# Attention and a feed-forward block in nine chunks: an earlier turn of the numerators, later operand splits

## The chip, the cores and the metric

The kernel runs on one core of a Trainium2 chip. The metric is device time in microseconds, from one launch to its end; lower is better. Inputs and outputs lie in device memory, and all arithmetic is in 32-bit floating point.

## The reference

Attention with two kinds of mask, followed by a layer norm, a feed-forward block and a residual:

```python
scores = scale * np.matmul(q, k.transpose(0, 1, 3, 2))      # 8 batches, 8 heads, 576 positions, 64
mask_local = (rel >= 0) & (rel < 32)                         # heads 0 to 3
mask_strided = (rel >= 0) & (pos[None, :] % 32 == pos[:, None] % 32)   # heads 4 to 7
attn = softmax(np.where(masks, scores, -1e9))
x = matmul(attn, v)                                          # as 8 x 576 x 512
xn = (x - mu) / np.sqrt(var + 1e-06) * g_ln
out = x + np.maximum(xn @ w_ch1, 0.0) @ w_ch2                # 512 -> 2048 -> 512
```

## The kernel before

**Chunks.** The 8 x 576 positions are worked on as nine chunks of 512, numbered 0 to 8. The feed-forward block has 16 feature blocks of 128. A factor of a matmul is kept as a high and a low part, so that a product costs three matmuls (high by high, high by low, low by high). Chunk 0 is computed while the weights are still being prepared, by a list of steps (`ORDER`). Chunks 1 and 2 are `plain`: for each feature block `f`, eight plus four matmuls into the PSUM tile `ph`, then ACT's `hh` (high part of the rectified sum), DVE's `hl` (low part), and *groups*, the second product, one group of three matmuls for each 128 positions, into the output banks `po`. Groups of a block run during the next block. The four output tiles of a chunk are two PSUM tiles of two outputs each; at a chunk's end DVE's four `finish` operations (line 901) scale and add them to the residual, and the next chunk takes the same banks. Chunks 3 to 6 are computed by `pair`: two feature blocks and two halves of the positions form a 2 x 2 block product, done with seven products (`a11 b11`, `s2 t2`, `s1 t1`, `a12 b21`, `s3 t3`, `a22 t4`, `s4 b22`), each of six matmuls of 256 columns, with a group behind each. The four sums of them (`u2`, `u3`, `p1`, line 1285) are made by DVE, and `Quarter` makes their rectified high (ACT) and low parts (DVE, `hq`). Eight pairs are one chunk. Chunks 7 and 8 end the kernel.

**Attention beside it.** A `Pair` is two heads of one batch, local or strided in turn. Its steps are woven into chunks 1 to 6, one *visit* for each pair of heads. In a visit TensorE computes the scores of the next pair (`nxt`) and the products with v of the present one (`now`); both use the same two PSUM tiles, `m` and `n`. DVE adds the mask and takes the maximum, POOL subtracts it (`s_sub`), ACT takes the exponent (`s_exp`). The result, the *numerators*, must be turned before it can be a matmul's factor: `p_turned` transposes blocks of 32 x 32 on DVE and writes them to device memory (`pd`) by four DMAs from SP, and `p_load` fetches them back as `pt`, by four DMAs from SP for strided pairs and one from ACT for local ones. The next visit's products with v read `pt`. Further steps of a visit: `v_store` writes the attention output (`xdl`, `xds`), `x_raw` fetches it back in blocks (`xraw`, from ACT), `load_v` fetches v for the pair after next, `t_piece` turns raw q and k (two transposes on DVE), and `load_qk` fetches the next raw q and k (`raw`, eight DMAs from SP, into the one tile that `t_piece` reads).

**What sets the order.** Each engine, and each DMA queue (SP's above all), does its instructions strictly in the order in which the program writes them. In chunks 1 and 2 the generator `pieces` cuts a visit in steps by `yield`; `plain` asks for four steps in each feature block, between `hl` of this block and the groups. So the first four steps of a visit stand in one block, the next four in the following one, and a visit takes three blocks (the last of a chunk takes four). In chunks 3 to 6 `pair` writes the steps out by hand between its products; the names P1, P6, P5, P2, P7, P4, P3 are the places behind the seven products, in that order. `events` does there what `X_AT` lists in the last pair (`last`) of chunks 3, 4 and 5: `x_split` makes the high (ACT) and low part (engine by `LO`) of each operand of the next chunk, as soon as its tile is free. An odd pair also turns raw q and k by `t_pieces`, one half at each `next(turns, None)`.

Of the kernel before, what the change touches and what calls it, by code (L numbers as in the profile page):

```python
# [63 lines left out]
def kernel(  # L64
# [10 lines left out]
    nc = tc.nc  # L75
# [235 lines left out]
    def bank(name):  # L311
        pool, tag, n = banks[n_bank[0] % len(banks)]
        n_bank[0] += 1
        return pool.tile([P, n], F32, tag=tag, name=name)
# [381 lines left out]
    def m_piece(p, nxt):  # L696

        name = (p or nxt).id
        ps = bank(f"m{name}"), third[0].tile([P, CH], F32, tag="h", name=f"n{name}")
        visits[0] += 1  # L700
        parts = nxt.s_blocks(ps) if nxt else None
        av = p.v_blocks(ps) if p else None
        if nxt:
            nxt.s_mask(parts)
        if p:
            p.v_divide(av[0:2])
        if nxt:
            nxt.s_max()
            nxt.s_sub()
            nxt.s_exp()  # L710
        if p:
            p.v_divide(av[2:])
            p.v_store()
# [16 lines left out]
    pairs = [Pair(b, hp) for b in range(B) for hp in order]  # L730
# [46 lines left out]
    def stage_x(name):  # L777
        if name not in staged_x:
            staged_x[name] = tkp.tile([P, 2, HC], F32, tag="tk", name=f"staged_{name}")
        return staged_x[name]  # L780

    def stage_sums(j):

        for out, x, y in (("t3", "b22", "t1"), ("t1", "t1", "b11"), ("t2", "b22", "t1"), ("t4", "b21", "t2")):
# [2 lines left out]

    OPERANDS = ("b11", "t2", "t1", "b21", "t3", "t4", "b22")
    LO = dict(b11=nc.vector, t2=nc.gpsimd, t1=nc.vector, b21=nc.gpsimd, t3=nc.gpsimd, t4=nc.gpsimd,
              b22=nc.vector)  # L790
    xs = {}

    def x_hi(name):
# [2 lines left out]
    def x_lo(name, eng=None):  # L796
        hi, lo = xs[name]
        (eng or LO[name]).tensor_tensor(out=lo, in0=stage_x(name), in1=hi.bitcast(F32), op=ALU.subtract)
        if name == "t4":
            del staged_x[name]  # L800

    def x_split(name):
        x_hi(name)
        x_lo(name)
# [292 lines left out]
    def pieces(i0, i1):  # L1097
        for i in range(i0, i1):
            now = pairs[i] if i >= 2 * NHP else None
            nxt = pairs[i + 1]  # L1100
            short = i not in (3 * NHP - 1, i1 - 1)
            soon = not nxt.local
            m_piece(now, nxt)
            yield
            yield
            yield
            yield
            if now and i < 4 * NHP:
                now.x_raw(nc.scalar)
            nxt.p_turned()  # L1110
            yield
            nxt.v_sums()
            if soon:
                nxt.p_load((nc.sync,))
            pairs[i + 2].load_v()
            yield
            pairs[i + 2].t_piece()
            yield
            pairs[i + 3].load_qk()
            yield  # L1120
            if not soon:
                nxt.p_load((nc.scalar,))
            yield
            if now and (now.b == 2 or i in (3 * NHP + 2, 3 * NHP + 3)):
                now.x_blocks()
            yield
            yield
            yield
            if not short:
                for _ in range(4):  # L1130
                    yield
# [139 lines left out]
    def product2(p, name, x, ps, start=True):  # L1271
        if name in slots:
            w = slots[name]
        else:
            w = high1[p] if name == "a22" else w1s[2 * p][:, :, HC * (int(name[2]) - 1):HC * int(name[2])]
        xh, xl = xs[x]
        for j in range(2):
            wh, wl = (w[:, i, P * j:P * (j + 1)] for i in range(2))
            for i, (wx, xx) in enumerate(((wh, xh), (wh, xl), (wl, xh))):
                nc.tensor.matmul(  # L1280
                    ps, wx, xx[:, j], start=(start and j == 0 and i == 0), stop=(j == 1 and i == 2),
                    skip_group_check=not start)
# [20 lines left out]
    def late_low():  # L1303
        if late:
            late.pop().low()
# [50 lines left out]
        (7, "P5"): [lambda: half_x(0, "b210", G, in_a(2))],  # L1356
        (7, "P7"): [lambda: half_x(0, "b211", V, (xb_t[1][:, 0], xb_t[1][:, 1]))],
    }
    X_AT = dict(P1=("b11",), P6=("t2",), P2=("b21",), P7=("t3",), P4=("t1", "t4"), P3=("b22",))

    def pair(c, p):
        even, last = p % 2 == 0, p == NFC // 2 - 1
        fin, entry = c == wide - 1, (c, p) == (FIRST, 0)
        n = NFC * (c - FIRST) + 2 * p
        i = NHP * (c + 1) + 1 + p // 2
        now, nxt, soon, far = (pairs[k] if k < NP else None for k in range(i, i + 4))
        off = 3

        def events(slot):
            if fin:  # L1370
                for do in final.get((p, slot), ()):
                    do()
            elif last:
                for name in X_AT.get(slot, ()):
                    x_split(name)

        if even and now:
            ps = bank(f"m{i}"), ps_b.tile([P, CH], F32, tag="h", name=f"n{i}")
            parts = nxt.s_blocks(ps) if nxt else None
            av = now.v_blocks(ps)  # L1380
            now.v_divide(av[0:2])
            if nxt:
                if not nxt.local:
                    parts[0:2] = parts[1], parts[0]
                nxt.s_mask(parts)
            now.v_divide(av[2:])
            now.v_store()
            if nxt:
                nxt.s_max()
        late_low()  # L1390
        if entry:
            x_lo("b22")
        x1 = ps_h.tile([P, CH], F32, tag="h", name=f"x1_{c}_{p}")[:, 0:HC]
        product2(p, "a11", "b11", x1)
        nc.scalar.copy(out=p1_t, in_=x1)
        events("P1")
        split_w(n + 1)
        if even and nxt:
            nxt.s_sub()
            if not entry:  # L1400
                nxt.s_exp()
        elif nxt:
            nxt.v_sums()
            nxt.p_load((nc.scalar, nc.sync))
        stage_w(n + 3)
        run_groups(1)
        x2 = ps_b.tile([P, CH], F32, tag="h", name=f"x2_{c}_{p}")[:, 0:HC]
        product2(p, "s2", "t2", x2)
        add2(u2_t, x2, p1_t)
        if entry:  # L1410
            x_lo("t4", nc.vector)
        turns = soon.t_pieces() if soon and not even else iter(())
        next(turns, None)
        if p == 1:
            pairs[NHP * (c + 1)].x_raw(nc.sync)
        events("P6")
        run_groups(1)
        x3 = bank(f"x3_{c}_{p}")[:, 0:HC]
        product2(p, "s1", "t1", x3)
        next(turns, None)  # L1420
        events("P5")
        run_groups(1)
        product2(p, "a12", "b21", x1, False)
        q = Quarter(c, 2 * p, 0, x1)
        q.low()
        split_w(n + 2)
        w_whole(NFC // 2 * (c - FIRST) + p)
        if entry:
            nxt.s_exp()
        elif even and nxt:  # L1430
            nxt.p_turned()
        stage_w(n + 4)
        events("P2")
        run_groups(1)
        product2(p, "s3", "t3", x2, False)
        add2(u3_t, x2, p1_t)
        add2(p1_t, x3, u3_t)
        q22 = Quarter(c, 2 * p + 1, 2, p1_t)
        if entry:
            nxt.p_turned()  # L1440
        if even and soon:
            soon.load_v()
        if even and now and p < NFC // 2 - 2:
            now.x_raw(nc.scalar, range(2))
        if far and not even:
            far.load_qk()
        events("P7")
        run_groups(1)
        x4 = (ps_h if even else ps_b).tile([P, CH], F32, tag="h", name=f"x4_{c}_{p}")[:, 0:HC]
        product2(p, "a22", "t4", x4)  # L1450
        add2(u3_t, x4, u3_t)
        q21 = Quarter(c, 2 * p + 1, 0, u3_t)
        q22.low()
        if 0 <= p - off < NT:
            res[c].append([x_load(c, p - off)])
        if even and now and p < NFC // 2 - 2:
            now.x_raw(nc.scalar, range(2, 4))
        if now and not even and not last:
            now.x_blocks()
            if p == 5 and not fin:  # L1460
                stage_sums(1)
        events("P4")
        run_groups(1)
        product2(p, "s4", "b22", x3, False)
        add2(u2_t, x3, u2_t)
        late.append(Quarter(c, 2 * p, 2, u2_t))
        q21.low()
        if 0 <= p - off - 1 < NT:
            k = p - off - 1
            res[c][k].append(x_scale(res[c][k][0], f"{c}_{k}"))  # L1470
        if p == 3:
            pairs[NHP * (c + 1)].x_blocks()
            if not fin:
                stage_sums(0)
        events("P3")
        run_groups(2)
# [99 lines left out]
    for f in range(NFC):  # L1576
# [4 lines left out]
        if f in (5, 6, 8, 9):  # L1581
            i = (5, 6, 8, 9).index(f)
# [5 lines left out]
    last = {}  # L1588
# [39 lines left out]
```

## Time and profile before

| | before |
|---|---|
| median of 3 runs | 884.07 us (881.9 to 884.26) |
| the profiled execution's own time | 882.23 us |
| its span | 880.4 us |
| TensorE busy | 860.8 us, 98% of the span |
| VectorE (DVE) busy | 555.0 us, 63% |
| ScalarE (ACT) busy | 282.8 us, 32% |
| GpSimd (POOL) busy | 369.9 us, 42% |

The span goes from the first to the last instruction. Busy time is not the same as useful time: matmuls overlap, so that a matmul that starts a little late may leave no gap in the busy time. Rows of a timeline give start and duration in us, the engine, the line of the kernel, the operation, the tile written and the tiles read, and, in brackets, how long the engine stood idle before and what ended that. Rows of waits give the total in us, the count, and the longest.

### The profile page before, as it was taken

How to read it: one execution, taken by the hardware profiler on the slowest of the kernel's cores; microseconds unless marked ns; L12 is line 12 of the kernel's file. 1: busy time of each engine (PE TensorE's matmuls, PEld its weight loads, DVE VectorE, ACT ScalarE, POOL GpSimd, SP SyncE). 2: the span in 40 equal slices, each digit the busy share in tenths (PEclk: the TensorE clock that was granted, in tenths of full speed). 3: DMA queues.
4: the chain of work that ended last, by engine and by line, in shares of the span. 5: the costliest groups of instructions: out<-in, count | busy, mean ns of one | idle time of the engine just before them, and what ended most of it. 6: DMA issues, size and time to landing. Idle time of an engine off the chain costs nothing.

```text
span 880.4 us, 20783 instructions
## 1 busy us (share of the span) xinstructions
PE 860.8 (98%) x7981; PEld 729.7 (83%) x7981; DVE 555.0 (63%) x1161; ACT 282.8 (32%) x588; POOL 369.9 (42%) x444
## 2 busy tenths in 40 slices
PE   6799999999999999999999999999999999999997
PEld 6678888888788888888888888888888888888886
DVE  6799994555555568676766776677866852434442
ACT  3686741111111114233432342334334421212121
POOL 4777852433333335245624452456437711212000
PEclk9799999999999999999999999999999999999999
DMA  9999853768868777979698978886774124321111
GB/s 189 189 293 273 249 110 88 154 161 168 169 169 158 181 167 177 215 183 190 164 207 196 194 175 209 182 172 157 174 176 118 49 96 137 102 85 48 55 41 48
DMA packets 374746, 137.99 MB, mean 157 GB/s; under 512 B 297204, under 2 KB 353144, under 8 KB 374648
## 3 DMA queue, kind: packets, MB, share of 16 engines
q1 hardware_dynamic: 317016, 125.00, 58.6%
q10 hardware_dynamic: 57632, 11.67, 7.2%
q8 instruction: 63, 1.03, 0.5%
q14 instruction: 35, 0.29, 0.1%
HBM read 99.58 MB, written 37.03 MB: 155 GB/s over the span
## 4 chain that ended last, share of the span: by engine, by line
PE 79%; DMA 7%; DVE 5%; SPq 4%; issue 2%; ACT 1%; POOL 1%; ACTq 1%; DVEq 0%; POOLq 0%
PE po L927 37%; PE x L1280 15%; PE x L1507 9%; PE ph L878 8%; PE ph L885 4%; PE m L454 2%; DMA pt<-pd 1%; SPq L362 1%; PE n L523 1%; DMA v_s<-in_v_dram 1%; SPq L651 1%; DMA xraw<-xds 1%; PE m L523 1%; DVE u L1285 1%; PE t L379 1%
## 5 line engine op out<-in xcount | busy, mean ns | idle before, releaser
L927 PE MATMUL po<-w,hq 128*128 128x512 f32 x768 | 213.7, 394 | 0.0
L927 PE MATMUL po<-w,hh 128*128 128x512 f32 x640 | 199.5, 393 | 0.0
L927 PEld LDWEIGHTS po<-w,hq 128*128 128x128 f32 x768 | 129.8, 189 | 14.3 <-issue 0.3
L927 PEld LDWEIGHTS po<-w,hh 128*128 128x128 f32 x640 | 118.1, 188 | 24.4 <-issue 0.2
L927 PE MATMUL po<-w,hl 128*128 128x512 f32 x320 | 124.8, 390 | 0.0
L1280 PE MATMUL x<-xh_b,w 128*128 128x256 f32 x512 | 113.1, 284 | 0.9 <-DVE u L1285 0.8
L1280 PEld LDWEIGHTS x<-xh_b,w 128*128 128x128 f32 x512 | 87.3, 188 | 10.9 <-DVE u L1285 5.7
L1222 POOL TENSOR_TENSOR w<-sw,w 128x256 fp32r<-128x256 f32 x64 | 52.1, 835 | 77.4 <-ACT w L1221 58.6
L895 DVE SCALAR_TENSOR_TENSOR hl<-ph,hh 128x512 fp32r<-128x512 f32 x48 | 33.0, 687 | 77.8 <-ACT hh L890 77.6
L500 POOL TENSOR_TENSOR sm<-sm,mx 128x640 f32<-128x640 f32 (+1 forms) x31 | 40.6, 1309 | 93.4 <-DVE mx L495 57.7
L878 PE MATMUL ph<-xh,w 128*128 128x512 f32 x188 | 74.6, 397 | 0.0
L753 POOL TENSOR_TENSOR rs<-rs,mhalf 128x1 f32<-128x1 f32 x36 | 22.3, 619 | 122.9 <-DVE rs L752 116.7
L878 PE MATMUL ph<-xl,w 128*128 128x512 f32 x188 | 73.4, 390 | 0.0
L1280 PE MATMUL x<-xl_b,w 128*128 128x256 f32 x256 | 71.8, 281 | 0.0
L927 PEld LDWEIGHTS po<-w,hl 128*128 128x128 f32 x320 | 60.1, 188 | 12.7
L890 ACT ACTIVATE hh<-ph 128x512 fp32r<-128x512 f32 x48 | 28.6, 597 | 115.1 <-PE ph L885 86.1
L1280 PEld LDWEIGHTS x<-xl_b,w 128*128 128x128 f32 x256 | 48.2, 188 | 4.7
L506 ACT ACTIVATE sm<-sm 128x648 f32<-128x648 f32 (+1 forms) x32 | 23.8, 744 | 84.5 <-POOL sm L500 70.3
L885 PE MATMUL ph<-xh,w 128*128 128x512 f32 x188 | 50.5, 391 | 0.0
L1172 POOL TENSOR_TENSOR rings<-stage,rings 128x512 fp32r<-128x512 f32 x14 | 18.1, 1292 | 74.5 <-ACT rings L1171 74.5
L1293 ACT ACTIVATE hq<-u 128x256 fp32r<-128x256 f32 x64 | 26.7, 417 | 60.1 <-DVE u L1285 22.0
L1222 POOL TENSOR_TENSOR xh_a<-sw,xh_a 128x256 fp32r<-128x256 f32 x32 | 24.3, 758 | 48.9 <-ACT xh_a L1221 48.9
(224 smaller groups left out, 1748.8 us busy)
## 6 DMA issues: line engine op xcount, KB each, us to landing
s<-in_moe_w_ch_dram SPq DMA_DIRECT2D x32, 512.0 KB
sw<-sd SPq DMA_DIRECT2D x64, 256.0 KB
out_dram<-x SPq DMA_DIRECT2D x32, 256.0 KB
raw<-in_q_dram SPq DMA_DIRECT2D x108, 72.0 KB
raw<-in_k_dram SPq DMA_DIRECT2D x108, 72.0 KB
xds<-xo SPq DMA_DIRECT2D x32, 162.0 KB
v_l<-in_v_dram SPq DMA_DIRECT2D x32, 144.0 KB
pd<-sm SPq DMA_DIRECT2D x48, 96.0 KB
```

The lines of the kernel that those rows point to most:

```text
L500: eng.tensor_tensor(out=sm, in0=sm, in1=mx[:, :, 0:nt].unsqueeze(3).broadcast_to([P, 2, nt, sm.shape[3]]), op=ALU.subtract)
L506: nc.scalar.activation(out=self.smv, in_=self.smv, func=AF.Exp, scale=SCALE)
L753: nc.gpsimd.tensor_tensor(out=rs, in0=rs, in1=mhalf, op=ALU.pow)
L878: nc.tensor.matmul(ph, w1h[:, cc], x[:, cc, :], start=(new and n == 0 and i == 0), stop=False)
L885: nc.tensor.matmul(ph, w1l[:, cc], xt[c][0][:, cc, :], start=False, stop=(cc == NCC - 1))
L890: nc.scalar.activation(out=hh, in_=ph, func=AF.Relu)
L895: nc.vector.scalar_tensor_tensor(out=hl, in0=ph, scalar=0.0, in1=hh.bitcast(F32), op0=ALU.max, op1=ALU.subtract)
L927: nc.tensor.matmul(po[c, i], hx, w, start=(n_po[c, i] == 0 and n == 0), stop=(n_po[c, i] == NFC - 1 and n == 2))
L1222: nc.gpsimd.tensor_tensor(out=w[:, 1], in0=t[:, k], in1=w[:, 0].bitcast(F32), op=ALU.subtract)
L1280: nc.tensor.matmul(ps, wx, xx[:, j], start=(start and j == 0 and i == 0), stop=(j == 1 and i == 2), skip_group_check=not start)
L1293: nc.scalar.activation(out=self.h[0], in_=src, func=AF.Relu)
L1507: nc.tensor.matmul(ps, wx, xx, start=(start and j == 0 and i == 0), stop=(j == 1 and i == 2), skip_group_check=not start)
```

## The change

In chunks 1 and 2 the numerators' turn and its four writes go from the visit's fifth step to its fourth, and so from the second feature block of the visit to its first. The fetch of strided numerators goes behind the v loads and one step later. In the last pair of chunks 3, 4 and 5 the second transposition of raw q and k goes from behind `s1 t1` to behind the sums that follow `s3 t3`; `t1` is split at P3 in place of P4, behind the last product; and the low part of `b22` is made by POOL in place of DVE there (at the entry to chunk 3 it stays on DVE).

```diff
     LO = dict(b11=nc.vector, t2=nc.gpsimd, t1=nc.vector, b21=nc.gpsimd, t3=nc.gpsimd, t4=nc.gpsimd,
-              b22=nc.vector)
+              b22=nc.gpsimd)
...
             yield
             yield
             yield
+            nxt.p_turned()
             yield
             if now and i < 4 * NHP:
                 now.x_raw(nc.scalar)
-            nxt.p_turned()
             yield
             nxt.v_sums()
+            pairs[i + 2].load_v()
+            yield
             if soon:
                 nxt.p_load((nc.sync,))
-            pairs[i + 2].load_v()
-            yield
             pairs[i + 2].t_piece()
...
-    X_AT = dict(P1=("b11",), P6=("t2",), P2=("b21",), P7=("t3",), P4=("t1", "t4"), P3=("b22",))
+    X_AT = dict(P1=("b11",), P6=("t2",), P2=("b21",), P7=("t3",), P4=("t4",), P3=("t1", "b22"))
...
         if entry:
-            x_lo("b22")
+            x_lo("b22", nc.vector)
...
         product2(p, "s1", "t1", x3)
-        next(turns, None)
+        if not last:
+            next(turns, None)
         events("P5")
...
         q22 = Quarter(c, 2 * p + 1, 2, p1_t)
+        next(turns, None)
```

The order of DVE in the first visit of chunk 1, one piece of the difference: L482 and L495 are mask and maximum, L633 the turn of the numerators `sm`, L901 the four `finish` of chunk 0, L895 `hl` of feature block 1.

```order
 L482 TENSOR_TENSOR sm_191<-m_2_2161,mask_s 64x54
 L495 TENSOR_REDUCE mx_2_2188<-sm_191 128x12
+L633 STREAM_TRANSPOSE sm_192<-sm_191 128x6x4x32
 L901 SCALAR_TENSOR_TENSOR x_0_1845<-po_0_992,rs_0_1888,x_0_1845 128x512
 L901 SCALAR_TENSOR_TENSOR x_1_1824<-po_0_992,rs_1_1877,x_1_1824 128x512
 L901 SCALAR_TENSOR_TENSOR x_2_1792<-po_2_999,rs_2_1818,x_2_1792 128x512
 L901 SCALAR_TENSOR_TENSOR x_3_1945<-po_2_999,rs_3_2092,x_3_1945 128x512
-L895 SCALAR_TENSOR_TENSOR hl_1_2227<-ph_1_2212,hh_1_2225 128x512
-L633 STREAM_TRANSPOSE sm_192<-sm_191 128x6x4x32
+L895 SCALAR_TENSOR_TENSOR hl_1_2232<-ph_1_2217,hh_1_2230 128x512
```

The turn has moved from behind `hl` to ahead of the four `finish`; chunk 2 begins in the same way.

The order of SP in a later visit of chunk 1 with strided scores to come, before: `xdl` is the attention output, `sd` the weight sums, `pd` the numerators' writes, `x` the residual, `pt` their fetch.

```order
L586 DMA xdl<-xo 128x4x128
L587 DMA xdl<-xo 64x128
L836 DMA sd<-f_1_2465 128x2x256
L837 DMA sd<-f_1_2468 128x512
L637 DMA pd_205<-sm_192 32x4x192 x4
L741 DMA x_1_2655<-xdl 128x256
L743 DMA x_1_2655<-xds 128x1x256
L651 DMA pt_3_2661<-pd_205 128x6x32 x4
L400 DMA v_l<-in_v_dram 32x17x64
L401 DMA v_l<-in_v_dram 32x18x64
```

The same place of SP now:

```order
L586 DMA xdl<-xo 128x4x128
L587 DMA xdl<-xo 64x128
L637 DMA pd_205<-sm_192 32x4x192 x4
L836 DMA sd<-f_1_2465 128x2x256
L837 DMA sd<-f_1_2468 128x512
L741 DMA x_1_2655<-xdl 128x256
L743 DMA x_1_2655<-xds 128x1x256
L400 DMA v_l<-in_v_dram 32x17x64
L401 DMA v_l<-in_v_dram 32x18x64
L400 DMA v_l<-in_v_dram 32x17x64
L401 DMA v_l<-in_v_dram 32x18x64
L651 DMA pt_3_2665<-pd_205 128x6x32 x4
```

The writes `pd` have passed the two `sd`, and the fetch `pt` stands behind the four v loads.

The order of DVE in the last pair of chunk 3, before: `qt_s` and `kt_s` are the two turns, `u`, `p` the sums, `hq` low parts, `xl_a` the low part of `t1`.

```order
L428 STREAM_TRANSPOSE qt_s<-raw_3_5255 128x18x32
L428 STREAM_TRANSPOSE kt_s<-raw_3_5255 128x18x32
L1296 SCALAR_TENSOR_TENSOR hq_14_0_5565<-x_3_7_5510,hq_14_0_5565 128x256
L1285 TENSOR_TENSOR u_2143<-x_3_7_5534,p_2141 128x256
L1285 TENSOR_TENSOR p_2141<-x_3_7_5548,u_2143 128x256
L1285 TENSOR_TENSOR u_2143<-x_3_7_5604,u_2143 128x256
L1296 SCALAR_TENSOR_TENSOR hq_15_2_5588<-p_2141,hq_15_2_5588 128x256
L798 TENSOR_TENSOR xl_a<-staged_3768,xh_a 128x512
L1285 TENSOR_TENSOR u_2142<-x_3_7_5548,u_2142 128x256
```

The same place of DVE now:

```order
L428 STREAM_TRANSPOSE qt_s<-raw_3_5255 128x18x32
L1296 SCALAR_TENSOR_TENSOR hq_14_0_5564<-x_3_7_5510,hq_14_0_5564 128x256
L1285 TENSOR_TENSOR u_2143<-x_3_7_5534,p_2141 128x256
L1285 TENSOR_TENSOR p_2141<-x_3_7_5548,u_2143 128x256
L428 STREAM_TRANSPOSE kt_s<-raw_3_5255 128x18x32
L1285 TENSOR_TENSOR u_2143<-x_3_7_5604,u_2143 128x256
L1296 SCALAR_TENSOR_TENSOR hq_15_2_5587<-p_2141,hq_15_2_5587 128x256
L1285 TENSOR_TENSOR u_2142<-x_3_7_5548,u_2142 128x256
L1296 SCALAR_TENSOR_TENSOR hq_15_0_5612<-u_2143,hq_15_0_5612 128x256
```

The second turn stands behind two sums, and the low part of `t1` has left the place ahead of the last sum.

## Rows read from the trace of the kernel before

**Rows 1.** Waits of PE, 140 to 345 us and 415 to 626 us.

```profile
PE n L523 <- DMA pt<-pd: 1.4, 2, 1.0
...
PE x L1280 <- DVE u L1285: 0.8, 3, 0.4
```

**Rows 2.** Timeline of PE in chunk 1: scores and first groups of two visits.

```profile
182.66 0.80 PE L454 MATMUL m<-kt_s,qt_s 64*64 64x54 f32 x40
...
184.40 0.74 PE L927 MATMUL po<-w,hh 128*128 128x512 f32 x2
...
219.24 0.80 PE L454 MATMUL m<-kt_s,qt_s 64*64 64x54 f32 x40
...
222.01 0.73 PE L927 MATMUL po<-w,hh 128*128 128x512 f32 x2
```

**Rows 3.** Chain of waits, followed back from 221 us: start, duration, what.

```profile
213.73 2.94 DMA xraw<-xds
...
216.69 4.38 DMA pt<-pd
```

**Rows 4.** Timeline of SP's DMA issues in chunk 1.

```profile
195.48 3.90 SPq L651 DMA_DIRECT2D pt<-pd  x4
199.42 0.54 SPq L400 DMA_DIRECT2D v_l<-in_v_dram  x1
...
205.21 3.03 SPq L362 DMA_DIRECT2D raw<-in_k_dram  x4
...
211.18 2.70 SPq L637 DMA_DIRECT2D pd<-sm  x4
```

**Rows 5.** Timelines of ACT and DVE in the same visit: exponent and turn.

```profile
206.42 0.74 ACT L506 ACTIVATE sm<-sm 128x640 f32<-128x640 f32 x1 [4.71 <-DMA raw<-in_q_dram]
...
209.77 0.83 DVE L633 STREAM_TRANSPOSE sm<-sm 128x640 f32<-128x640 f32 x1
```

**Rows 6.** Timelines of DVE, ACT and PE in the first visit of chunk 1.

```profile
150.04 2.72 DVE L901 SCALAR_TENSOR_TENSOR x<-po,rs,x 128x512 f32<-128x512 f32 x4
...
154.88 0.97 DVE L633 STREAM_TRANSPOSE sm<-sm 128x768 f32<-128x768 f32 x1
...
151.51 0.75 ACT L506 ACTIVATE sm<-sm 128x648 f32<-128x648 f32 x1 [3.83 <-POOL sm L500]
...
153.38 0.61 PE L927 MATMUL po<-w,hh 128*128 128x512 f32 x2
```

**Rows 7.** Timeline of PE at the end of chunk 3: groups, product, scores.

```profile
423.77 0.86 PE L927 MATMUL po<-w,hq 128*128 128x512 f32 x3
...
425.18 0.86 PE L927 MATMUL po<-w,hq 128*128 128x512 f32 x3
...
426.47 0.39 PE L1280 MATMUL x<-xh_b,w 128*128 128x256 f32 x1 [0.44 <-DVE u L1285]
...
427.29 0.86 PE L927 MATMUL po<-w,hq 128*128 128x512 f32 x3
...
428.69 1.55 PE L927 MATMUL po<-w,hq 128*128 128x512 f32 x6
...
430.35 0.80 PE L454 MATMUL m<-kt_s,qt_s 64*64 64x54 f32 x40
...
432.90 0.86 PE L927 MATMUL po<-w,hq 128*128 128x512 f32 x3
...
434.50 0.86 PE L927 MATMUL po<-w,hq 128*128 128x512 f32 x3
```

**Rows 8.** Timelines of DVE and POOL in the same place.

```profile
424.58 1.25 DVE L428 STREAM_TRANSPOSE kt_s<-raw 128x576 f32<-128x576 f32 x1
...
430.21 1.17 DVE L1296 SCALAR_TENSOR_TENSOR hq<-u,hq 128x256 fp32r<-128x256 f32 x1
...
432.31 0.68 DVE L798 TENSOR_TENSOR xl_b<-staged,xh_b 128x512 fp32r<-128x512 f32 x1
...
429.55 1.55 POOL L798 TENSOR_TENSOR xl_b<-staged_t,xh_b 128x512 fp32r<-128x512 f32 x1
```

## The prediction

> **What bounds the kernel now.** I read the page's busy shares first, then TensorE's waits, then single instructions around each wait. TensorE is busy for 98% of the span and the other engines for 63% or less, so an edit pays only where a matmul starts later than its predecessor allows. Behind the first chunk there are few such places: the waits show two for `pt<-pd` in chunks 1 and 2 (1.4 us together), and three for `u` in chunks 3 to 5 (0.8 us together) [rows 1]. Recorded waits understate the loss, since matmuls overlap, so below I compare starts: from one fixed matmul to the next, against the same distance where nothing is late.
>
> **Chunks 1 and 2: what the earlier turn saves.** In an undisturbed visit the strided scores start at 182.66 and the groups behind the visit at 184.40: 1.74 us. In the visit of the long wait it is 219.24 to 222.01, 2.77 us, so 1.03 are lost [rows 2]. The visit at 299.00 has the same pattern with 2.25 us and loses 0.51. Together 1.54 us.
>
> The chain back from that wait is `xds` store, `xraw` (ends at 216.67), local numerators `pt` from 216.69 to 221.07 [rows 3]. Its start is SP: it was still issuing `raw` loads up to 208.24 and came to the four `pd` writes only at 211.18 [rows 4]. They had been ready earlier: the exponent ended at 207.16, the turn started at 209.77, behind the next feature block's `hl` [rows 5]. Now the turn follows the exponent at once, 2.6 us earlier, and the writes stand ahead of `sd` and `xraw`. In strided visits SP no longer sits in the numerators' fetch (3.9 us for four issues, [rows 4]) while the v loads queue behind it, so the `raw` loads end earlier too and the next `xds` store and `xraw` follow. The fetch of `pt` takes 4.4 us and is late by 1.0; the turn alone gives its writes 2.6. I take the whole 1.54 us, with 0 as the other end.
>
> What is moved past: four `pd` writes go ahead of two `sd` writes, so these leave some 2 us later. They free POOL's weight-sum tiles; POOL stands idle for much of these chunks (42% busy over the span), so I cost that at nothing. It would cost something if POOL came late to a visit's subtraction, since the turn now keeps DVE waiting for it. In ordinary visits `hl` is not delayed: the turn now runs from 207.2 to 208.0, and `hl`, some 0.7 us long, ended only as the old turn began at 209.77 [rows 5]. In the visit of chunk 2 with operand transposes behind the turn the same check leaves `hl` some 0.4 us late, which the twelve matmuls of groups before its PSUM bank is written again cover.
>
> **Chunks 1 and 2: what it costs.** A chunk's first visit differs. There DVE has also the four `finish` operations, which empty the output banks of the chunk before, and they stood ahead of the turn; the order shows them behind it now. In front they ran at 150.04, four in 2.72 us, in the very time in which POOL and ACT made the exponent. Now DVE waits for the exponent (ends at 152.26), turns (0.97), and only then finishes at 0.68 each. The first group of the new chunk writes the bank of the first two: 152.26 + 0.97 + 2 x 0.68 = 154.59, where TensorE wanted it at 153.38 [rows 6]. That is 1.2 us of new wait. The next two finishes end at 155.95, and TensorE asks at 154.59 + 1.36 = 155.95: no second wait. `hl` is done some 0.7 later, before its bank is wanted. The same sum at the next chunk's first visit (a local one, turn 0.84, exponent to 250.25, groups at 251.40) gives 1.05. Together **+2.3 us**. Bounds: 0 if the groups don't wait for both finishes, 2.7 if latencies of 0.2 are added at each.
>
> **The last pair of chunks 3, 4, 5.** Both turns of the next raw tile (the second at 424.58, 1.25 us) stand ahead of DVE's `u` sums [rows 8]. The product a22·t4 writes the PSUM tile that the sum reads, and waits. From group to group with one product between it is 1.41 us undisturbed (423.77 to 425.18) and 2.11 here (425.18 to 427.29): 0.70 lost [rows 7]. Chunks 4 and 5 show the same pair of rows with 1.83 and 1.81: 0.42 and 0.40. Together 1.52. With the second turn behind both sums this goes: they are free about 1.1 us earlier, and the largest loss is 0.7. What is late next is a22's own sum, behind the turn; only the next visit's tile needs it, over 1 us later. The eight `raw` loads wait for the turn also, some 0.7 us later on SP; no one needs them for a pair.
>
> At the chunk's end, t1's low part (a wait for ACT, then 0.9) stood ahead of the sum that frees the bank for the visit's scores. They start 1.66 us after the last two groups (428.69 to 430.35), where other visits show 1.48: 0.18 lost, in each of three chunks, 0.54 together [rows 7]. b22's low part at 432.31 then delays the visit's reading, and the group-to-group distance is 1.60 (432.90 to 434.50) for 1.41: 0.19, three times, 0.57 [rows 7, 8]. With t1 behind the sum and b22 on POOL, DVE has one subtraction fewer there. Together 1.52 + 0.54 + 0.57 = **2.6 us** saved; bounds 0.5 (only part of the first) and 2.6. A gain above it is excluded, since nothing more is lost in these places. Operands are wanted later than they come: t1 in the third product of the next pair, b22 in its last.
>
> On POOL against DVE the rows speak against the move: `hq` took 1.17 us at 430.21, while the same instruction takes 0.41 to 0.42 elsewhere, and POOL was in t4's subtraction (429.55, 1.55 us) [rows 8]. The Trainium skill (SBUF — State Buffer, section "SBUF: two separate sides") says that a DVE instruction with two SBUF inputs and a GpSimd instruction that reads SBUF take a port as an exclusive lock, one blocking for all of the other's time. The trace agrees in direction (0.75 us added). By that rule t1's subtraction may now wait out one of POOL's.
>
> **The sum.** 2.3 - 1.5 - 2.6 = -1.9 us. The profiled execution's own time is 882.23 (span 880.4), so 880.3 for a like one. It lies 1.8 below the median of 884.07, within its runs (881.9 to 884.26); on the median the forecast is **882.2**. That is 0.2%. About 0.3% (2.7 us) is what a measurement of this kernel can tell from no change.
>
> **The rivals.**
> - *The chunk starts cost nothing* (the finishes stay in time, because the exponent comes sooner or one finish is enough): -4.2 us, 879.9. For it: DVE idles before `hl` there. Against it: the exponent's end is in the rows, and the bank holds two outputs. Chance 0.15.
> - *The `pt` waits stay*, because the local fetch follows `xraw` and not the writes: in the chain it starts 0.02 us after `xraw` ends [rows 3]. Then 2.3 - 2.6 = -0.3, 883.8. Chance 0.14.
> - *The last pairs gain nothing*: another reader of the same bank is late in place of the sum, as happens at 0.15 us in an odd pair that is not changed. 2.3 - 1.5 = +0.8, 884.9. The edit would not do what it says. Chance 0.10.
> - *DVE is blocked by POOL at the chunk's end*: t1's subtraction, due at about 429.9, waits out 1.5 us of POOL and ends as the visit starts; the third loss of 0.57 stays. -1.3, 882.7. Chance 0.08. This is what the SBUF page's rule would do here.
> - *Slower: strided numerators come too late.* Their fetch stands behind four v loads, each about 0.55 us of issue [rows 4], and stood ahead of them. If the writes' lead does not bring SP to it earlier, it ends 2.2 us later, and four of the five strided visits (the fifth has a feature block to spare) stall TensorE for up to that: +8.8 - 1.9, 891.0. It decides once the fetch's last issue ends later than 2 us before the products that read it; in rows 4 it ended at 199.38, and no wait of that visit is among rows 1. Against it: the turn is 2 to 3 us earlier, which pays for the v loads. Chance 0.08.
>
> **How the numbers follow.** The forecast has 0.45, the rivals 0.55 as above. The range for 8 in 10: down to the first rival and 0.6 for the spread of the runs (879.3), up to the third with a little spread (885.2); what lies outside is the slower case and the tails. Faster by over 0.3% (below 881.4): most of the first rival (0.13) and a quarter of the forecast (0.11), 0.24. Slower: the last rival and a tail, 0.09. Within: 0.67.
>
> **What would show it.** Right: no wait for `pt<-pd` in chunks 1 and 2, distances of 1.74 in all strided visits; two new waits of the first groups of chunks 1 and 2 for DVE's `finish` (line 901), 1.2 and 1.05 us; group distances near 1.41 in the last pairs, and only the unchanged pair's small wait for `u` left. Wrong: new waits for `pt` behind strided visits, `hl` late in ordinary visits, waits of DVE for POOL at chunk ends, or two starts of chunks without a gap.

## The result, and the profile after

The changed kernel takes 895.03 us, median of 6 runs (893.57 to 897.32); the kernel before took 883.42 beside it (6 runs, 880.96 to 884.26). The ratio is 1.0138, 95% interval 1.0117 to 1.0159: 12 us slower, where I forecast 2 us faster. The profiled execution took 893.57 us, 11.3 more than that of before (882.23), and its span is 891.8.

The head of the page (busy time per engine; then TensorE's busy tenths in 40 slices of the span):

```profile
PE 863.0 (97%) x7981; PEld 730.5 (82%) x7981; DVE 556.1 (62%) x1158; ACT 283.0 (32%) x588; POOL 373.0 (42%) x447
...
PE   7799999998998989999999999999999999999997
```

Apart from the first two slices and the last, TensorE's row has three below 9, all between 200 and 340 us (before it had none), so the loss lies in chunks 1 and 2 and in three places. Waits of PE from 140 to 350 us (compare the first of [rows 1]; each line gives what was waited for, us in total, times, longest):

```profile
PE n L523 <- DMA pt<-pd: 8.3, 6, 2.5
PE po L927 <- DVE x L901: 2.2, 2, 1.2
```

The second line was forecast. The first should have been empty; it has grown from 1.4 to 8.3 us, and the visits have changed: the two late ones of before had local numerators, and these go with `v_s`, so they are strided. Timeline of PE at the first two of them and at the third (start, duration, instruction, the wait ahead of it):

```profile
204.72 0.30 PE L523 MATMUL n<-v_s,pt 54*64 54x64 f32 x2 [2.17 <-DMA pt<-pd]
205.72 0.24 PE L523 MATMUL n<-v_s,pt 54*64 54x64 f32 x1 [0.58 <-DMA pt<-pd]
206.46 0.79 PE L927 MATMUL po<-w,hh 128*128 128x512 f32 x2
...
289.65 0.30 PE L523 MATMUL n<-v_s,pt 54*64 54x64 f32 x2 [2.46 <-DMA pt<-pd]
290.61 0.24 PE L523 MATMUL n<-v_s,pt 54*64 54x64 f32 x1 [0.54 <-DMA pt<-pd]
...
329.00 0.29 PE L523 MATMUL n<-v_s,pt 54*64 54x64 f32 x2 [1.84 <-DMA pt<-pd]
330.09 0.33 PE L523 MATMUL n<-v_s,pt 54*64 54x64 f32 x1 [0.67 <-DMA pt<-pd]
```

By the yardstick of the prediction (from the start of the scores to the first group, 1.74 to 1.76 in an undisturbed visit) the three take 4.88, 5.13 and 5.18 us: 3.1 + 3.4 + 3.4 = 9.9 us lost. From these scores to the next ones the three are longer than before by 4.73, 3.34 and 4.30 us, 12.4 together: another 2.4 us are lost behind two of the stalls. The granted clock shows where. Behind the first and the third, but not the second (290 to 295 us), TensorE ran part of the time at 1.2 instead of 2.4 GHz (stretches of 5 us: length, busy us of PE, PEld, DVE, ACT, POOL, then PEclk, DMA share, GB/s):

```profile
200.00:205.00 5.00, 2.83 (x84) 2.15 (x82) 0.69 (x1) 0.60 (x1) 0.00 (x0) 1.00 0.80 117
205.00:210.00 5.00, 4.42 (x52) 3.51 (x51) 2.74 (x9) 0.00 (x0) 1.10 (x1) 0.70 0.75 121
210.00:215.00 5.00, 5.00 (x22) 4.09 (x21) 1.31 (x2) 1.34 (x2) 1.56 (x3) 0.96 0.59 156
290.00:295.00 5.00, 4.46 (x58) 3.72 (x57) 2.74 (x9) 0.00 (x0) 1.21 (x1) 1.00 0.70 113
325.00:330.00 5.00, 2.58 (x82) 1.84 (x80) 0.69 (x1) 0.60 (x1) 0.31 (x1) 0.99 0.86 132
330.00:335.00 5.00, 4.91 (x52) 4.13 (x53) 2.74 (x9) 0.00 (x0) 1.25 (x2) 0.67 0.62 102
```

Why the fetch is late is in the chain of waits behind the first stall (start, duration, what; SPq is SP issuing a DMA):

```profile
190.95 2.42 DMA xraw<-xdl
...
193.44 0.38 SPq L836
...
195.51 0.53 SPq L400
...
197.16 1.93 SPq L401
...
199.13 1.13 SPq L651
...
202.44 3.15 DMA pt<-pd
```

SP had issued the `pd` writes early. Then it stood 0.8 us, until an `xraw` transfer had landed, before it issued `sd` (L836); it passed `x` and the four v loads, the last of which took 1.93 us, and began the fetch (L651) at 199.13. Before, it began at 195.48 [rows 4]. The writes and the fetch in SP's timeline, here and (last line) the writes of the kernel before:

```profile
190.56 2.04 SPq L637 DMA_DIRECT2D pd<-sm  x4
...
199.13 4.59 SPq L651 DMA_DIRECT2D pt<-pd  x4
```

```profile
192.50 1.79 SPq L637 DMA_DIRECT2D pd<-sm  x4
```

The writes left 1.9 us earlier than before, and the fetch started 3.65 us later and its four issues took 0.69 longer. (The scores of this visit start 0.64 us later than before, 201.58 against 200.94, so against them the lead is 2.6 and the delay 3.0 us.) The lead went nowhere.

At the other edits: the first groups of chunks 1 and 2 wait for `finish` (L901), as forecast (PE):

```profile
153.91 0.70 PE L927 MATMUL po<-w,hh 128*128 128x512 f32 x2 [1.17 <-DVE x L901]
...
256.87 0.70 PE L927 MATMUL po<-w,hh 128*128 128x512 f32 x2 [1.05 <-DVE x L901]
```

From the scores across a last pair to the next scores it took 24.03, 23.75 and 23.79 us before, and 23.27, 23.24 and 23.26 now: 1.80 us gained in chunks 3 to 5. The stretch behind each, with the first pairs of the next chunk, took 23.30, 23.28 and 23.31, and takes 23.42, 23.42 and 23.44 now: 0.39 lost.

### The profile page after: what moved, and what is told of

It reads as the page before. It is cut to its first block, busy times and chain, and to the rows that moved or that the text cites. A ratio compares the mean times of both kernels' runs of the same rounds, so it can differ in the third digit from the quotient of the medians.

```text
span 891.8 us, 20777 instructions
## 1 busy us (share of the span) xinstructions
PE 863.0 (97%) x7981; PEld 730.5 (82%) x7981; DVE 556.1 (62%) x1158; ACT 283.0 (32%) x588; POOL 373.0 (42%) x447
## 4 chain that ended last, share of the span: by engine, by line
PE 86%; DMA 4%; SPq 3%; DVE 2%; issue 2%; POOL 1%; ACT 1%; ACTq 0%; POOLq 0%; DVEq 0%
PE po L927 41%; PE x L1280 18%; PE x L1509 9%; PE ph L878 7%; PE ph L885 4%; PE m L454 2%; PE n L523 1%; SPq L651 1%; DMA pt<-pd 1%; PE m L523 1%; SPq L401 1%; DMA v_l<-in_v_dram 1%; POOL sm L500 1%; DMA s<-in_moe_w_ch_dram 1%; DMA pd<-sm 1%
## 5 line engine op out<-in xcount | busy, mean ns | idle before, releaser
L927 PE MATMUL po<-w,hh 128*128 128x512 f32 x640 | 201.6, 397 | 2.2 <-DVE x L901 2.2
L895 DVE SCALAR_TENSOR_TENSOR hl<-ph,hh 128x512 fp32r<-128x512 f32 x48 | 32.9, 686 | 64.1 <-ACT hh L890 64.1
```

Source lines behind the costliest of these rows:

```text
L895: nc.vector.scalar_tensor_tensor(out=hl, in0=ph, scalar=0.0, in1=hh.bitcast(F32), op0=ALU.max, op1=ALU.subtract)
L927: nc.tensor.matmul(po[c, i], hx, w, start=(n_po[c, i] == 0 and n == 0), stop=(n_po[c, i] == NFC - 1 and n == 2))
```

## The experiments

The theory after the result: the fetch's place behind the v loads alone makes the three stalls. Rivals: the early `pd` writes crowd SP and the DMA queues, whatever stands where; or `sd`, now between writes and fetch (where only `x` stood before), does it.

### The fetch put back ahead of v

```
             nxt.v_sums()
+            if soon:
+                nxt.p_load((nc.sync,))
             pairs[i + 2].load_v()
             yield
-            if soon:
-                nxt.p_load((nc.sync,))
```

> The changed kernel with one thing undone: SP again issues the strided numerators' fetch ahead of the four v loads. The early turn and the edits of the last pairs stay. Theory (the fetch stands behind v on SP and so ends late): the three waits for the numerators of 1.8 to 2.5 us go, with them about 9.9 us of late groups and about 2.5 us of lower clock behind them; what is left of the change is +2.7 (two chunk starts), -1.6 (old waits for the numerators gone), -1.3 (last pairs), so about 883 us, within 1 us of the kernel before. Rival (the early writes, ahead of the sd and x transfers, crowd the queues and make the fetch late): the stalls stay, 892 us or more.

Measured: 881.84 us (12 runs), ratio to before 0.9971, interval 0.9954 to 0.9988. Waits of PE from 140 to 350 us, and SP in chunk 1:

```profile
PE po L927 <- DVE x L901: 2.2, 2, 1.2
PE n L523 <- DMA pt<-pd: 1.0, 2, 0.6
```

```profile
194.84 3.78 SPq L651 DMA_DIRECT2D pt<-pd  x4
198.66 0.54 SPq L400 DMA_DIRECT2D v_l<-in_v_dram  x1
```

The stalls are gone and the early writes acquitted. But the fetch starts at 194.84, only 0.64 us earlier than before, though its writes left 2.7 us earlier (189.83). With `sd` in between (0.8 us of waiting for `xraw` and 0.9 us of issues), most of the turn's lead doesn't reach the fetch. That lead could not have paid for the v loads. Against the kernel before the ratio is 2.6 us of gain, where I had expected next to none; this is taken up below.

### The kernel before with the fetch alone moved

The reverse: only the fetch moves behind v, the turn stays late.

> The kernel before with one thing done: the strided fetch stands behind the four v loads; the turn stays in its late place. Theory (the place behind v makes it late): the fetch ends at least as late as in the changed kernel, since its writes leave 2 us later; three to four visits stall by 3 to 6 us each, and the time is 893 to 905 us. Rival (only early writes crowd the queues): no new wait, 883 to 885 us.

Measured: 895.13 us (4 runs), ratio 1.0127, interval 1.0101 to 1.0153. As slow as the whole change, by this one move. Waits of PE from 140 to 350 us, and SP's fetch in chunk 1:

```profile
PE n L523 <- DMA pt<-pd: 8.7, 7, 2.7
```

```profile
198.25 4.12 SPq L651 DMA_DIRECT2D pt<-pd  x4
```

The early turn bought these three visits little: scores to groups take 5.06, 4.66 and 5.83 us, much as in the changed kernel. Only the first strided visit of chunk 1 stalls here and not there (2.54 us, 0.8 lost).

### Without the v loads ahead of the fetch

In the changed kernel, `if not soon:` ahead of `pairs[i + 2].load_v()`. This kernel leaves the four v loads out, so its local pairs use old values of v and its result is not the attention; it serves for the time alone.

> The changed kernel without the four v loads that stand ahead of the strided fetch: in chunks 1 and 2, the v tiles of the local pairs keep the values of the batch before (that part of the computation is changed). Theory (the v loads' issues on SP make the fetch late): its last issue comes 3 to 4 us earlier, the three waits of 1.8 to 2.5 us go, 882 to 884 us. Rival (the sd and x transfers between the writes and the fetch, and the wait of sd for an earlier transfer, make it late): most of the stalls stay, 890 us or more.

Measured: 881.04 us (10 runs), ratio 0.9957, interval 0.9941 to 0.9974, and no wait for `pt` from 140 to 350 us. The fetch begins at 194.63 and ends its issues at 198.58:

```profile
194.63 3.95 SPq L651 DMA_DIRECT2D pt<-pd  x4
```

`sd` still stands in front of it, and the fetch still stands one step later than before. So the second rival falls too, and so does the later step: the four v loads make the stalls.

### The fetch issued by ACT

`p_load((nc.scalar,))` in place of `p_load((nc.sync,))`, at the place of the changed kernel.

> The changed kernel with the strided fetch issued by ACT instead of SP, at the same place of the program; the v loads stay on SP. Theory (only SP's order of issue makes the fetch late): it no longer queues behind v, the waits for the numerators fall to under 1 us, and ACT pays with four issues of some 0.5 us in each of five visits beside its own work, which has 283 us in 892: 881 to 884 us. Rival (v loads and fetch share the DMA engines and their transfers collide): the fetch starts earlier but takes longer, waits of 1 to 2 us stay, 886 to 892 us.

Measured: 884.88 us (10 runs), ratio 1.0005, interval 0.9986 to 1.0024. The stalls are gone here as well (0.4 us for `pt`), which confirms SP's order as the cause. The price is on ACT (its timeline) and, behind it, PE:

```profile
309.87 4.70 ACTq L651 DMA_DIRECT2D pt<-pd  x4
314.67 0.60 ACT L890 ACTIVATE hh<-ph 128x512 fp32r<-128x512 f32 x1 [7.62 <-DMA pt<-pd]
```

```profile
316.04 0.50 PE L878 MATMUL ph<-xh,w 128*128 128x512 f32 x1 [1.53 <-DVE hl L895]
```

Four issues hold ACT for 4.7 us here, so `hh` starts late, `hl` with it, and the next feature block waits. I had taken an issue at 0.5 us; in this visit it is 1.2, and over the five visits the four take 3.03 to 4.70 us. By the ratios this costs about 3 us against the fetch put back ahead of v, and the time lies just above the range of my theory.

### The turn late again at the chunk starts

The changed kernel, with `p_turned` behind the finishes for `i in (7, 12)` only.

> The changed kernel with the turn in its old place in the first visits of chunks 1 and 2 alone, behind the four finish operations. Theory (the turn ahead of the finishes costs 1.5 and 1.2 us at the chunk starts): the two waits for the finishes of 1.17 and 1.05 us go, -2.7 us against the changed kernel, 892.3 us, since the first strided visit has time to spare. Rival (the first strided visit then stalls on its fetch as the three others do, +3.3): 895.5 us.

Measured: 894.95 us (4 runs), ratio 1.0119, interval 1.0094 to 1.0145; against the changed kernel's 1.0138 no clear gain, so my theory missed. The waits for `finish` are gone, and the two stretches behind them are shorter (18.84 to 17.38 us, 19.62 to 18.31: 2.8 us). In the profiled executions more than that, 4.9 us, is given back in the other stretches of the two chunks, nearly all in the visits that read strided numerators:

```profile
PE n L523 <- DMA pt<-pd: 9.8, 7, 2.6
...
163.83 0.24 PE L523 MATMUL n<-v_s,pt 54*64 54x64 f32 x1 [0.84 <-DMA pt<-pd]
```

The first strided visit now stalls too (2.81 us from scores to groups, 1.06 lost), and the others take 5.21, 5.57 and 5.75 instead of 4.88, 5.13 and 5.18: 2.4 us more of stalls, and the other 2.5 lie behind them. My reading, which no run separates: while the transfer is the last to arrive, an earlier start of TensorE only makes it wait longer. My rival had the place right and the price too high: 1.1 us there, the rest in the other visits.

### The last pairs alone

The kernel before with the second turn behind two sums, `t1` and `b22` split later, and `b22` on POOL; and the same with `b22` on DVE.

> The kernel before with the edits of the last pairs alone (second turn behind two sums, t1 and b22 split later, b22 on POOL). Read from the two traces: -2.3 us in the last pairs, +0.9 in the first pair of the chunks behind them, so -1.3 to -1.4 us, about 882 us. Rival (the loss in the first pairs comes from somewhere else in the change, such as the shifted phase of the weights' loads): -2.3 us and no loss there, 881.2 us.

> As the edits of the last pairs alone, but b22's low part stays on DVE. Theory (b22 on POOL pushes POOL's weight split and the visit's subtraction back, and so the product s4*b22 of the next pair by 0.3 us each): that loss goes, 0.9 us; in exchange DVE has b22 there again, which in the kernel before cost 0.19 us three times (0.57). So -2.3 + 0.6 = -1.7 us against before, 0.3 us faster than with b22 on POOL. Rival (POOL has no part in it): the loss of 0.9 stays and the 0.57 comes back, -0.8 us.

Measured: 883.35 us, ratio 0.9987 (0.9964 to 1.0010), and 883.88, ratio 0.9994 (0.9975 to 1.0013), 12 runs each. The times don't separate the two from each other or from the kernel before; the stretches do:

| from scores to scores, us | across the last pairs | behind them |
|---|---|---|
| before | 24.03, 23.75, 23.79 | 23.30, 23.28, 23.31 |
| changed kernel | 23.27, 23.24, 23.26 | 23.42, 23.42, 23.44 |
| last pairs alone, b22 on POOL | 23.25, 23.24, 23.27 | 23.43, 23.44, 23.60 |
| last pairs alone, b22 on DVE | 23.27, 23.24, 23.31 | 23.72, 23.71, 23.72 |

The first column repeats: about 1.8 us, whatever else is in the kernel. In the second, both versions lose, in different places. With `b22` on POOL (changed kernel, chunk 4; POOL, ACT and PE in turn):

```profile
445.07 1.28 POOL L798 TENSOR_TENSOR xl_b<-staged,xh_b 128x512 fp32r<-128x512 f32 x1
...
448.17 1.27 POOL L500 TENSOR_TENSOR sm<-sm,mx 128x648 f32<-128x648 f32 x1
```

```profile
449.47 0.75 ACT L506 ACTIVATE sm<-sm 128x648 f32<-128x648 f32 x1 [3.44 <-POOL sm L500]
450.13 0.36 ACT L1293 ACTIVATE hq<-x 128x256 fp32r<-128x256 f32 x1
```

```profile
451.85 0.85 PE L927 MATMUL po<-w,hq 128*128 128x512 f32 x3
453.53 1.55 PE L927 MATMUL po<-w,hq 128*128 128x512 f32 x6
```

POOL does `b22` first, then the weight split, then the visit's subtraction; the exponent and `hq` follow late, and the product s4·b22 waits: 1.68 us between the groups at 451.85 and 453.53 instead of 1.41. Three chunks lose 0.27, 0.32 and 0.31 there. With `b22` on DVE (the same places of PE):

```profile
437.23 0.86 PE L927 MATMUL po<-w,hq 128*128 128x512 f32 x3
439.26 0.86 PE L927 MATMUL po<-w,hq 128*128 128x512 f32 x3
...
444.89 0.86 PE L927 MATMUL po<-w,hq 128*128 128x512 f32 x3
446.30 1.55 PE L927 MATMUL po<-w,hq 128*128 128x512 f32 x6
```

The late product is back at 1.41 (444.89 to 446.30), so POOL was its cause. But the first distance is 2.03 where it was 1.60 before [rows 7]: DVE now does `t1` and `b22` one after the other ahead of the visit's reading. I had priced that at the old 0.19; moving `t1` there made it 0.62. In both kernels the product behind that distance starts 0.14 us after DVE has read the visit's tile `n` (433.57 and 438.33), so DVE's queue ahead of the reading is the cause. Part of that queue is an `hq` that takes 1.18 us beside a subtraction of POOL, where 0.42 is usual (in the kernel before one takes 1.17 there); those 0.76 us are more than the 0.62 lost, so by this estimate POOL has a share here too, which no run separates. By the stretches, `b22` is better off on POOL, the reverse of what I expected.

### The parts that pay, together

The early turn except for `i in (7, 12)`, the fetch ahead of v, the last pairs with `b22` on POOL.

> The parts that pay, together: the turn early except in the first visits of chunks 1 and 2, the strided fetch ahead of v as before, the edits of the last pairs with b22 on POOL. Theory: the changed kernel with the fetch put back (881.8 in its run, 0.9971 of before) less 2.7 us of chunk starts: about 5 us under the kernel before, 0.994 of it, near 879.5 us, with no wait of TensorE for a finish. Rival (the early turns themselves gain nothing and the earlier run only lay well): 0.998 of before, as the edits of the last pairs alone.

Measured: 880.00 us (6 runs, 878.43 to 880.87) against 884.39 of before beside it; ratio 0.9948, interval 0.9927 to 0.9968. Faster than both kernels, and near the 0.994 that I expected. Waits of PE from 140 to 350 us:

```profile
PE n L523 <- DMA pt<-pd: 1.4, 2, 0.9
```

Two small waits for `pt` remain and none for `finish`.

### Why the early turn may be worth more than it seemed

The last pairs alone give 1.1 us by their ratio (0.9987) and all paying parts 4.6 (0.9948): so the early turn would give about 3.5 us, or 2.5 by the medians (the ratios on record are not quite the quotients of the medians), where the trace of before showed 1.5. The two ratios' intervals leave this open from about 1 to 6 us. The trace of before was a good execution (882.23 us; the medians of before in the two later series are 885.22 and 884.39). The two kernels with the last pairs alone have the program of before in chunks 1 and 2. From the first scores of chunk 1 to the first product of chunk 3 the profiled executions took:

| kernel | us |
|---|---|
| before | 191.58 |
| last pairs alone, b22 on POOL | 193.86 |
| last pairs alone, b22 on DVE | 198.70 |
| changed kernel | 205.07 |
| fetch put back (with 2.7 us of chunk starts) | 194.10 |
| the parts that pay | 191.65 |

Up to 7 us lie between executions of the same code. The slowest waits for the same local numerators as [rows 2], only for longer (PE, `b22` on DVE):

```profile
221.26 0.24 PE L523 MATMUL n<-v_l,pt 64*32 64x64 f32 x1 [2.29 <-DMA pt<-pd]
222.16 1.20 PE L927 MATMUL po<-w,hh 128*128 128x512 f32 x2
```

Its first groups behind the stall take 1.20 us, where [rows 2] has 0.73 and 0.74: the lower clock again (granted 0.72 from 220 to 225 us). In the six profiled executions with the early turn no wait at a local visit of chunks 1 and 2 is over 0.5 us; but the kernel with the fetch alone moved, whose turn is late, has none either, so the turn is not the only thing that removes them. The six runs of the last kernel lie within 2.4 us, the 23 of before beside it within 7.0 (881.49 to 888.46). Why the transfers differ from run to run isn't settled.

## Why the prediction was wrong, and where it was right

| term of the sum, us | forecast | changed kernel |
|---|---|---|
| waits for local `pt` go | -1.5 | -1.56 |
| two chunk starts | +2.3 | +2.7 |
| strided fetch behind v | 0 (rival: +8.8) | +9.9, and +2.4 of clock |
| across the last pairs | -2.06 | -1.80 |
| behind the last pairs | -0.57 | +0.39 |
| ahead of chunk 1 (not changed) | 0 | -0.8 |

The measured terms sum to 11.2; the profiled executions differ by 11.3.

- **The step that failed** is the sentence "the turn is 2 to 3 us earlier, which pays for the v loads". The writes did leave 1.9 us earlier. But the same move that put them ahead of `sd` put `sd` between them and the fetch, with 0.8 us in which SP stood until an `xraw` transfer had landed. I asked what the writes' move does to `sd` and POOL, and never what `sd` does to the fetch. With the fetch put back, the lead that arrives is 0.64 us, against 3.6 us for four v loads (195.51 to 199.09 in the chain). I had taken 2.2, read where the loads stood behind the fetch; ahead of it the fourth one takes longer.
- **The slack was in my own rows.** I wrote that it decides 2 us before the products that read the fetch, and that the last issue ended at 199.38. Those products stood 0.9 us behind the scores at 200.94 (PE, kernel before):

```profile
201.84 0.27 PE L523 MATMUL n<-v_s,pt 54*64 54x64 f32 x1
```

That is a slack of 0.46 us, which I didn't work out. The runs agree: with the last issue 1.6 us ahead of the scores nothing was lost (before), with 1.9, 2.1 and 2.3 us behind them 3.3, 3.1 and 3.5 (fetch alone moved, changed kernel, starts late). If each us of delay costs one, the point of no loss is 1.0 to 1.4 us ahead of the scores, where a slack of 0.46 puts it at 1.1. In the changed kernel the last issue came 3.7 us later against the scores than before; less the slack that is 3.2, and the first stall lost 3.1. "No wait of that visit is among rows 1" was taken for room and was not.
- **The slower rival** had mechanism, place and nearly the price (+8.8 against 9.9 in the stalls; three visits at 3.3 instead of four at 2.2), and a chance of 0.08 that should have been far larger. It lacked the clock: two of the three stalls were followed by a stretch at the lower one.
- **Chunk starts**: right, 1.46 and 1.24 for 1.2 and 1.05. The two waits are 1.17 and 1.05 us; the gaps are a little longer, as the upper bound of 2.7 had it. The rival that they cost nothing falls. Removing them from the changed kernel gained nothing that its runs show, and lengthened the stalls.
- **Local `pt` waits**: right for the profiled execution (1.56), but its trace is one draw; over many runs the early turn may be worth about twice that. The rival that they stay, since the fetch follows `xraw`, falls.
- **Across the last pairs**: right in kind. The three gaps ahead of a22·t4 shrank by 0.61, 0.33 and 0.31 instead of 0.70, 0.42 and 0.40, because 1.50 us remain between groups where I had hoped for 1.41; the scores gained 0.18 each, as forecast.
- **Behind the last pairs**: the 0.57 came as 0.51, and 0.90 was lost on POOL. I had costed `b22` there at nothing, since "operands are wanted later than they come". That holds for the operand; what suffers is the work queued behind it on POOL.
- **DVE blocked by POOL**: not where I put it. `t1`'s subtraction (444.00, 0.69 us) fell between two of POOL's and was not longer for it. Two `hq` did meet one each (DVE and POOL at the end of chunk 3):

```profile
440.27 1.36 DVE L1296 SCALAR_TENSOR_TENSOR hq<-p,hq 128x256 fp32r<-128x256 f32 x1
...
441.89 1.18 DVE L1296 SCALAR_TENSOR_TENSOR hq<-u,hq 128x256 fp32r<-128x256 f32 x1
```

```profile
438.80 2.54 POOL L798 TENSOR_TENSOR xl_b<-staged,xh_b 128x512 fp32r<-128x512 f32 x2
441.46 1.32 POOL L798 TENSOR_TENSOR xl_b<-staged_t,xh_b 128x512 fp32r<-128x512 f32 x1
```

They end at 441.63 and 443.07, 0.29 us behind POOL's subtractions (441.34 and 442.78), and take 0.42 where POOL is idle. This is what the Trainium skill (SBUF — State Buffer, section "SBUF: two separate sides") says of a DVE instruction with two SBUF inputs against a GpSimd one that reads SBUF: whoever starts first holds the port for its whole instruction. The trace agrees. In the changed kernel it cost TensorE next to nothing: the first distance behind is 1.43 us for 1.41.

## What to carry to other kernels

Before a transfer is moved behind others on its queue, work out its slack from the row where its reader starts, and count what the queue must pass between the event that frees it and its issue, with the waits in there; a wait that doesn't show is not a margin. An early start on one engine is worth only what reaches the last arrival: look for what stands between on the same queue. And where waits for transfers are small in one profile, they may be several times larger in the next run of the same code, so an edit that relieves them can be worth more than the trace says.

## What the runs showed of the hardware

- Behind two stalls of TensorE that cost 3.1 and 3.4 us the granted clock was 0.70 and 0.67 of full over 5 us; behind a third of 3.4 us it stayed at 1.00. The lower clock went with a further loss of 1.6 and 0.9 us, the full one with none. The same matmul in the slow stretch and behind it (PE, changed kernel):

```profile
207.05 0.63 PE L927 MATMUL po<-w,hl 128*128 128x512 f32 x1
...
210.68 0.40 PE L927 MATMUL po<-w,hl 128*128 128x512 f32 x1
```

- One issue of the strided fetch held its engine for 0.6 to 1.3 us (four took 2.25 to 5.30 us on SP and 3.03 to 4.70 on ACT), where most v loads took 0.5.
- The fourth v load took 1.1 to 2.3 us on SP in all twelve visits behind the first of chunk 1 in which the v loads stood ahead of the fetch (changed kernel, fetch alone moved, starts late); in the kernel before the fourth took 0.3 to 0.7. While it ran the DMA engines' share was 1.24, 1.18 and 1.23 in chunk 1 of the three kernels, and 0.99 over the last two v loads of before. That the two go together is all that the runs show; the cause was not tested.
